# Lightning attention and mixture of depths on one core: who issues the second batch's stores, when the first fetch goes out, and in which order two score rows are compared

## The chip, the core and the metric

The kernel runs on one core of a Trainium2 chip. A core has five engines with instruction streams of their own: TensorE (PE in the profile; PEld is its loading of weights), VectorE (DVE), ScalarE (ACT), GpSimd (POOL) and SyncE (SP, which here only issues DMAs). They meet through semaphores. Each engine works through its own stream in order. The metric is the device time of one execution in microseconds, the median of the runs.

## The reference

The inputs are q, k and v of shape (4 batches, 8 heads, 768 positions, 64), a decay per head, a gate vector of 512, two weight matrices (512 x 1024 and 1024 x 512) and a capacity of 128.

```
for each block of 64 positions:
    out = ((q @ k.T) * Dmask) @ v  +  (q * lam_pow) @ kv_state
    kv_state = lam_block * kv_state + (k * rev_pow).T @ v
x = out with the heads side by side           # (4, 768, 512)
scores = x @ w_gate
for each batch: the 128 positions of highest score
    x[those] += sigmoid(scores) * (relu(x[those] @ w1) @ w2)
```

## The kernel before

**Tiling.** The 768 positions of a batch are six tiles of 128, so there are 24 tiles, numbered g = 0 to 23; batch 0 has tiles 0 to 5, batch 1 tiles 6 to 11, and so on. The main loop (L686) has one step for each tile, after a step -1. A step works on several tiles at once: it transposes q and k of tile g + 1 (`transposes`, L204, copied from PSUM by ScalarE at L208), multiplies the queries by the decay on GpSimd (`queries_decayed`, tile qs, L215 or L217), forms the scores of tile g + 1 (`scores`), the products of keys and values for the state (`state_products`, L279 or L288), the part of the output that comes from the state (`from_states`, L330 or L341) and the part that comes from the scores of tile g (`from_scores`, L357 or L364). ScalarE copies the outputs into the tile x_b (L386, or L392 and L394), which holds a whole batch. Steps up to 10 are "wide" (blocks of 128 positions at a time); from 11 on they are narrow (two blocks of 64), and they have time on TensorE for the experts' matrices (`expert`: L536, L572, L584), in pieces.

**Choosing the tokens.** `gate_scores` makes the score of each position on VectorE (xg, sc). `row` (L434 to L439) turns a tile's scores into a row: TensorE transposes them into a PSUM bank, ScalarE copies the row into sc_row in SBUF. `compare` (L441) counts on VectorE which scores beat which: a first comparison, `beat` (L447), reads `fresh[g]`; a second, `table` (L456), reads the rows of the earlier tiles from sc_row; L461 adds the two up. `column_sums` adds up the tables on TensorE (L473) and takes the result off the ranks (L477). Two steps after the end of a batch, `find` makes `hit` (L489), in which each position's rank is compared with the 128 places. `tokens` turns this into row numbers: six small matmuls on TensorE (L499) and two VectorE instructions (L504, L506). `fetch` (L523) is an indirect DMA, issued by GpSimd, that reads those 128 rows back from the output in HBM. `take` does both. The results of the experts are written over those rows by another indirect DMA (L602, L607).

**What sets the order.** The order in which instructions are given to each engine is written out by hand: it is the order of the calls. A row, a transposed tile and the products of L279 each take the next of four PSUM banks (`bank`), in turn, so a bank is written again only when the last reader of what it held is done. In steps 3 to 7 the dictionary `ROWS` says which rows are handled; step 7 takes two, those of tiles 5 and 6. Tile 6 is the first of its batch, so its comparison has no `table`. The row of a tile is therefore read twice by others than TensorE: by ScalarE's copy and by `beat`.

**DMAs.** SyncE issues all loads of k, q and v (L76, three for a tile, four to eight tiles ahead) and, in steps 8 to 13, the weights (L94 and L99). ScalarE issues the stores of finished tiles (L399), at the end of the steps that the dictionary `STORES` gives: tiles 6 and 7 in step 11, 8 and 9 in step 12, 10 and 11 in step 13. The framework gives DMAs of these two engines eight completion semaphores in turn, in an order over both engines. A DMA is issued only when the DMA that last used its semaphore has landed; that can be one of the other engine.

Of the kernel before, what the change touches and what calls it, by code (L numbers as in the profile page):

```python
# [17 lines left out]
def kernel(  # L18
# [12 lines left out]
    nc = tc.nc  # L31
# [5 lines left out]
    L = 128  # L37
    C = 64
    NT = S // L
# [103 lines left out]
    o_ = psum.tile([128, 2, 512], FP32, name="o")  # L143
    free = [psum.tile([128, 512], FP32, name=f"m{i}") for i in range(4)]
    held = []
    ROWS = {1: (), 2: (), 3: (0,), 4: (1, 2), 5: (3,), 6: (4,), 7: (5, 6)}
    KEPT = range(NG)
    STORES = {
        3: [0], 4: [1, 2], 5: [3, 4], 6: [5], 11: [6, 7], 12: [8, 9], 13: [10, 11], 18: [12, 13], 19: [14, 15], 20: [16, 17],
# [28 lines left out]
    def wide(g):  # L178
        return g < WIDE
# [44 lines left out]
    def scores(g, part=None):  # L224
        if g >= NG:
            return
        hps = range(NHP) if part is None else range(part * NHP // 2, (part + 1) * NHP // 2)
        qT, kT = qTs[g], kTs[g]
        if part != 0:
            qTs.pop(g), kTs.pop(g)  # L230
        if wide(g):
            to = o_ if part == 1 else su
            for hp in hps:
                for hh in range(2):
                    nc.tensor.matmul(  # L235
                        to[:, hh, hp * L : (hp + 1) * L], lhsT=kT[half[hh], hp, :],
                        rhs=qT[half[hh], hp, :], start=True, stop=True, skip_group_check=True,
                    )
            return
        for hp, hh, c in quarters():  # L240
            nc.tensor.matmul(  # L241
                su[half[c], hh, hp * C : (hp + 1) * C], lhsT=kT[half[hh], hp, half[c]],
                rhs=qT[half[hh], hp, half[c]], start=True, stop=True, skip_group_check=True,
            )
# [49 lines left out]
    def decay_state(n):  # L294
        g = n // 2
        if g >= NG or n % (2 * NT) == 0 or n % (2 * NT) == 2 * NT - 1:
            return
        if wide(g) and g % NT == NT - 1:
            return
        t = att.tile([128, NHP, D], FP32, name="decayed", bufs=2)  # L300
        nc.gpsimd.tensor_tensor(  # L301
            out=t[:], in0=states[n][:], in1=(decay_w if wide(g) else decay)[:], op=ALU.mult
        )
        decayed[n] = t
# [91 lines left out]
    def store(g):  # L396
        for n in STORES.get(g, [] if g in KEPT else [g]):
            b, t = divmod(n, NT)
            nc.scalar.dma_start(  # L399
                out=out[b, t * L : (t + 1) * L, :],  # L400
                in_=x_bs[b][:, t].rearrange("p a b e -> p (a b e)"),
            )
# [22 lines left out]
    def row(g):  # L425
        if not 0 <= g < NG:
            return
        b, t = divmod(g, NT)
        if t == 0:
            rows_[b] = mod.tile([128, S], FP32, name="sc_row")  # L430
            same_[b] = mod.tile([128, NT], FP32, name="same")
            prev_[b] = mod.tile([128, NT], FP32, name="prev")
            ranks[b] = mod.tile([128, NT], FP32, name="ranks")
        pb = bank()[:, :L]  # L434
        nc.tensor.transpose(  # L435
            pb, in_=scs[b][:, t : t + 1].broadcast_to([128, 128]), identity=ident[:]
        )
        nc.scalar.copy(out=rows_[b][:, t * L : (t + 1) * L], in_=pb)  # L438
        fresh[g] = pb  # L439

    def compare(g):  # L441
        if not 0 <= g < NG:
# [52 lines left out]
    def tokens(b, i):  # L495
        e = hits_.pop((b, i))
        pk = bank()[:, :2]
        for t in range(NT):
            nc.tensor.matmul(  # L499
                pk, lhsT=e[:, t, :], rhs=place[:, b * NT + t, :],  # L500
                start=(t == 0), stop=(t == NT - 1),
            )
        two = mod.tile([128, 2], FP32, name="two")
        nc.vector.tensor_copy(two[:], pk)  # L504
        tok = const.tile([128, 1], I32, name=f"tok{b}_{i}")
        nc.vector.scalar_tensor_tensor(  # L506
            out=tok[:], in0=two[:, 0:1], scalar=128.0, in1=two[:, 1:2],
            op0=ALU.mult, op1=ALU.add,
        )
        toks[b, i] = tok  # L510
# [10 lines left out]
    def fetch(b, i):  # L521
        xs = mod.tile([128, HD], FP32, name="xs")
        nc.gpsimd.indirect_dma_start(  # L523
            out=xs[:], out_offset=None, in_=rows_upto(b), in_offset=rows_at(b, i),
        )
        xss[b, i] = xs
# [142 lines left out]
    def ends(g):  # L669
        return g >= 0 and g % NT == NT - 1  # L670
# [5 lines left out]
    def take(b):  # L676
        for i in range(NGR):
            tokens(b, i)
            fetch(b, i)
# [6 lines left out]
    for g in range(-1, NG):  # L686
        loads_to(g + ahead(g), g)
        if g < 0:
            keys_decayed(0)
        if wide(g):  # L690
            if NGR:
                pending = list(tables)
                for n in ROWS.get(g, (g - 1,)):
                    row(n)
                    compare(n)
                for n in pending:
                    column_sums(n)
                if ends(g - 4):
                    take((g - 4) // NT)
            if g < 0:  # L700
                for part in range(2):
                    transposes(0, "kT", part)
                    transposes(0, "qT", part)
                for part in range(2):
                    scores(0, part)
                    masked(0, part)
                query_powers()
            elif g == 0:
                transposes(1, "kT")
                from_scores(0, 0)  # L710
                transposes(1, "qT")
                from_scores(0, 1)
                outputs(0)
                store(0)
                queries_decayed(1)
                nc.scalar.copy(
                    out=decay_w[:], in_=qpow[:, :, L - 1 : L].broadcast_to([128, NHP, D])
                )
                decay_state(2)
            else:  # L720
                for name in ("kT", "qT") if g == 1 else ("qT", "kT"):
                    transposes(g + 1, name)
                queries_decayed(g + 1)
                from_scores(g)
                outputs(g)
                store(g)
                if g > 1:
                    gate_scores(g)
            if g == 0:
                scores(1)  # L730
            if g != 1:
                state_products(g + 1)
            if g > 0:
                scores(g + 1)
            if wide(g + 1):
                from_states(g + 1)
            if g == 1:
                masked(g + 1)
                state_products(g + 1)
            if g < 0:  # L740
                keys_decayed(1)
                constants()
            else:
                keys_decayed(g + 2)
            if g == 0:
                masked(1)
            next_state(2 * g + 2)
            if g >= 0:
                decay_state(2 * g + (3 if not wide(g + 1) else 4))
            if g > 1:  # L750
                masked(g + 1)
            if g == 1:
                nc.scalar.copy(
                    out=wg_o[:].rearrange("p (a b e) -> p a b e", a=2, e=D),
                    in_=wg_b[:].rearrange("p (b a e) -> p a b e", a=2, e=D),
                )
            if g in (1, 2):
                gate_scores(g - 1)
            second(g + 1)
            if g == 3:  # L760
                casts()
                narrow_constants()
            if NGR and ends(g - 2):
                column_sums(g - 2)
                find((g - 2) // NT)
        else:
            transposes(g + 1, "qT")
            transposes(g + 1, "kT")
            if ends(g - 6):
                for i in range(NGR):  # L770
                    pieces.extend(expert((g - 6) // NT, i))
            products(1)
            from_states(g)
            settle(g)
            queries_decayed(g + 1)
            state_products(g + 1)
            next_state(2 * g + 2)
            decay_state(2 * g + 3)
            keys_decayed(g + 2)
            if NGR:  # L780
                column_sums(g - 2)
                if ends(g - 4):
                    take((g - 4) // NT)
                row(g - 1)
            products(1)
            second(g + 1)
            if NGR:
                compare(g - 1)
                if ends(g - 2):
                    find((g - 2) // NT)  # L790
            products(1)
            flush()
            from_scores(g)
            scores(g + 1)
            outputs(g)
            store(g)
            masked(g + 1)
            gate_scores(g)
# [55 lines left out]
```

## Time and profile before

| | |
|---|---|
| Median of 3 runs | 179.09 us (177.38 to 180.19) |
| The profiled execution, its own time | 178.91 us |
| Its span | 177.1 us |
| TensorE busy | 162.2 us (92%) |
| VectorE busy | 98.2 us (55%) |
| GpSimd busy | 85.6 us (48%) |
| ScalarE busy | 69.0 us (39%) |
| Moved by DMA | 32.20 MB in 82608 packets, mean 182 GB/s |
| Of these on SyncE's queue | 23.34 MB, 61.3% of 16 engines' span |
| On ScalarE's queue | 6.30 MB, 10.6% |
| On GpSimd's queue | 2.10 MB, 3.7% |

The profile is of one execution. A group of instructions is named by engine, line, the tile written and the tiles read. In the chain of waits each piece of time is put on what the last instruction of all was waiting for, step by step backwards; "issue" there is time in which the engine waited for nothing that the profile shows. In the timeline a line has the start, the duration, the engine, the line of the kernel, the operation with its tiles and sizes and, in brackets, how long the engine was idle before it and what ended that. ACTq, SPq and POOLq are instructions that the sequencer of the engine handles itself, such as issuing a DMA. A line of 40 digits shows how busy something was in 40 equal slices of the span, in tenths.

The narrow step 11 begins at about 60 us, step 12 at 67, step 13 at 74, step 14 at 81, step 15 at 89 and step 16 at 97 us, if a step's first transposes are taken as its beginning.

### The profile page before, as it was taken

Reading aid. Unit: us, or ns where it says so; the run is one execution under the profiler, and the core shown is the slowest. Engines: PE = TensorE matmul, PEld = TensorE weight load, DVE = VectorE, ACT = ScalarE, POOL = GpSimd, SP = SyncE. Lnnn points to the kernel's source line nnn. Section 1 sums busy time; section 2 is a strip of 40 time slices with the busy share of each in tenths; the row PEclk is TensorE's granted clock in tenths of the full one; section 3 lists DMA queues with packets and bytes.
Section 4 is the critical chain, followed back from the end, with each engine's and each line's share of the span. In section 5 each row is a group of like instructions: output and inputs, shape, how many; then the busy total and the mean of one; then the engine's idle time right before and its main releaser. Section 6 shows DMA issues by size and latency. Waiting matters only on the chain.

```text
span 177.1 us, 7473 instructions
## 1 busy us (share of the span) xinstructions
PE 162.2 (92%) x3228; PEld 133.9 (76%) x3228; DVE 98.2 (55%) x304; ACT 69.0 (39%) x173; POOL 85.6 (48%) x96
## 2 busy tenths in 40 slices
PE   7999899998998988999688999899998999999990
PEld 7788798886987877896365699787655699559970
DVE  2873479699885547545255668547565767030011
ACT  3345366444332623543521465545334353013100
POOL 1386965265459660863567564836856300202022
PEclk9999999999999999999999999999999999999998
DMA  4999999999999999899998999972134242201000
GB/s 106 224 225 215 198 235 241 251 277 240 220 222 269 299 254 246 275 311 254 276 258 188 249 233 210 199 186 82 44 122 130 103 155 95 63 0 59 0 30 30
DMA packets 82608, 32.20 MB, mean 182 GB/s; under 512 B 75792, under 2 KB 77840, under 8 KB 82576
## 3 DMA queue, kind: packets, MB, share of 16 engines
q1 hardware_dynamic: 78320, 23.34, 61.3%
q10 hardware_dynamic: 3600, 6.30, 10.6%
q0 software_dynamic: 656, 2.10, 3.7%
q8 instruction: 25, 0.41, 1.0%
q14 instruction: 7, 0.06, 0.1%
HBM read 24.38 MB, written 7.34 MB: 179 GB/s over the span
## 4 chain that ended last, share of the span: by engine, by line
PE 63%; issue 9%; DMA 8%; SPq 7%; POOL 6%; DVE 3%; ACT 2%; POOLq 1%; ACTq 1%; DVEq 0%
PE m L572 14%; PE m L584 12%; PE m L204 9%; SPq L76 5%; PE o L341 4%; PE o L357 4%; PE su L241 4%; DMA qn<-in_q_dram 4%; PE o L364 4%; DMA kn<-in_k_dram 4%; PE su L288 3%; PE su L235 2%; PE o L330 2%; PE m L435 2%; POOL kd L186 2%
## 5 line engine op out<-in xcount | busy, mean ns | idle before, releaser
L572 PE MATMUL m<-xsT,w_sb 128*128 128x128 f32 x256 | 31.4, 276 | 0.2 <-ACT kT L208 0.2
L572 PEld LDWEIGHTS m<-xsT,w_sb 128*128 128x128 f32 x256 | 29.9, 192 | 1.0 <-ACT xsT L541 0.6
L584 PE MATMUL m<-w_sb,hs 128*128 128x512 f32 (+1 forms) x80 | 30.1, 508 | 0.0
L217 POOL TENSOR_TENSOR qs<-qT,qpow 128x512 f32<-128x512 f32 x13 | 16.6, 1280 | 24.5 <-ACT qT L208 24.5
L301 POOL TENSOR_TENSOR decayed<-state,decay 128x256 f32<-128x256 f32 x21 | 16.7, 794 | 6.8 <-DVE ranks L477 6.4
L208 ACT COPY qT<-m 128x512 f32<-128x512 f32 (+1 forms) x25 | 14.2, 569 | 14.4 <-PE m L204 8.9
L584 PEld LDWEIGHTS m<-w_sb,hs 128*128 128x128 f32 x80 | 14.2, 193 | 5.6 <-issue 4.8
L320 DVE TENSOR_TENSOR state<-su,decayed 128x256 f32<-128x256 f32 x21 | 8.9, 424 | 14.4 <-POOL decayed L301 10.3
L438 ACT COPY sc_row<-m 128x128 f32<-128x128 f32 x24 | 6.2, 268 | 27.3 <-PE m L435 20.1
L208 ACT COPY kT<-m 128x512 f32<-128x512 f32 (+1 forms) x25 | 14.3, 573 | 6.4 <-PE m L204 6.1
L204 PE MATMUL m<-ident,qn 128*128 128x128 f32 x96 | 15.8, 285 | 0.7 <-DMA qn<-in_q_dram 0.7
L255 DVE TENSOR_TENSOR p<-su,mask_w 128x1024 f32<-128x1024 f32 (+1 forms) x11 | 12.9, 1171 | 5.4 <-PE su L235 5.4
L576 ACT ACTIVATE hs<-m 128x128 f32<-128x128 f32 x32 | 8.9, 279 | 17.8 <-PE m L572 17.3
L186 POOL TENSOR_TENSOR kd<-kn,kpow_w 128x512 f32<-128x512 f32 x11 | 11.4, 1041 | 8.7 <-DVE kpow_w L117 5.2
L204 PE MATMUL m<-ident,kn 128*128 128x128 f32 x96 | 15.2, 279 | 0.5 <-DVE beat L447 0.2
L215 POOL TENSOR_TENSOR qs<-qT,qpow 128x512 f32<-128x512 f32 x9 | 11.5, 1277 | 8.5 <-ACT qT L208 8.4
L186 POOL TENSOR_TENSOR kd<-kn,kpow 128x512 f32<-128x512 f32 x13 | 13.5, 1039 | 0.0
L241 PE MATMUL su<-qT,kT 64*64 64x64 f32 x416 | 10.1, 221 | 3.4 <-issue 1.7
L357 PE MATMUL o<-vn,p 128*64 128x64 f32 x352 | 12.9, 225 | 0.2 <-DVE p L255 0.2
L357 PEld LDWEIGHTS o<-vn,p 128*64 128x64 f32 x352 | 11.3, 138 | 2.2 <-issue 1.9
L204 PEld LDWEIGHTS m<-ident,kn 128*128 128x128 f32 x96 | 11.2, 143 | 1.6 <-DVE beat L447 1.1
L235 PE MATMUL su<-qT,kT 64*128 64x128 f32 x168 | 12.3, 285 | 0.1
(86 smaller groups left out, 271.6 us busy)
## 6 DMA issues: line engine op xcount, KB each, us to landing
vn<-in_v_dram SPq DMA_DIRECT2D x24, 256.0 KB, 5.4
out_dram<-x_b ACTq DMA_DIRECT2D x24, 256.0 KB, 4.1
kn<-in_k_dram SPq DMA_DIRECT2D x23, 256.0 KB, 5.7
qn<-in_q_dram SPq DMA_DIRECT2D x23, 256.0 KB, 6.4
w_sb<-in_moe_w_dram SPq DMA_DIRECT2D x4, 512.0 KB, 6.5
w_sb<-in_moe_w_dram SPq DMA_DIRECT2D x8, 256.0 KB, 5.8
kn<-in_k_dram SPq DMA_DIRECT2D x2, 128.0 KB
qn<-in_q_dram SPq DMA_DIRECT2D x2, 128.0 KB
```

Source lines behind the costliest of these rows:

```text
L186: nc.gpsimd.tensor_tensor(out=kd[:], in0=loaded[g][0][:], in1=pw[:].rearrange("p a b -> p (a b)").unsqueeze(2).broadcast_to([128, H, D]), ...
L204: nc.tensor.transpose(tp[:, hp * L : (hp + 1) * L], in_=t[:, 2 * hp : 2 * hp + 2, :], identity=ident[:])
L208: nc.scalar.copy(out=dsts[g][:].rearrange("p a i -> p (a i)")[:, at], in_=tp[:, at])
L215: nc.gpsimd.tensor_tensor(out=qs[:], in0=qTs[g][:], in1=qpow[:], op=ALU.mult)
L217: nc.gpsimd.tensor_tensor(out=qs[:].rearrange("p a (c i) -> p a c i", c=2), in0=qTs[g][:].rearrange("p a (c i) -> p a c i", c=2), in1=qpow ...
L235: nc.tensor.matmul(to[:, hh, hp * L : (hp + 1) * L], lhsT=kT[half[hh], hp, :], rhs=qT[half[hh], hp, :], start=True, stop=True, skip_group_ ...
L241: nc.tensor.matmul(su[half[c], hh, hp * C : (hp + 1) * C], lhsT=kT[half[hh], hp, half[c]], rhs=qT[half[hh], hp, half[c]], start=True, stop ...
L255: nc.vector.tensor_tensor(out=ps_[g][:, :, at], in0=(o_ if part == 1 else su)[:, :, at], in1=mask_w[:].rearrange("p a b i -> p a (b i)")[: ...
L301: nc.gpsimd.tensor_tensor(out=t[:], in0=states[n][:], in1=(decay_w if wide(g) else decay)[:], op=ALU.mult)
L357: nc.tensor.matmul(o_[half[c], hh, hp * D : (hp + 1) * D], lhsT=p[:, hh, i0 : i0 + C], rhs=vn[:, 2 * hp + hh, :], start=(hp == 0 and g % N ...
L572: nc.tensor.matmul(ph, lhsT=w1_sb[:, dc, f * 128 : (f + 1) * 128], rhs=keep["xsT"][:, dc, :], start=(dc == 0), stop=(dc == NDC - 1),)
L584: nc.tensor.matmul(py[:, e0:e1], lhsT=keep["hs"][:, f, :], rhs=w2_sb[:, f, e0:e1], start=(f == 0), stop=(f == NFC - 1),)
```

## The change

Three things are changed.

- The stores of batch 1 (tiles 6 to 11, in steps 11, 12 and 13) are issued by SyncE, in the same places of the written order. In SyncE's stream each pair stands after the weights of its step and before the loads of the next.
- `tokens` of batch 0 moves from the beginning of step 9 to step 8, behind the step's outputs and gate scores and ahead of its state products; `fetch` of batch 0 moves from the beginning of step 9 to step 8, after `decay_state`, which makes it the last thing that GpSimd does in that step. For the later batches `take` stays where it was.
- In step 7 row 6 is handled before row 5, and for these two rows `beat` reads ScalarE's copy in SBUF and no longer the PSUM bank.

```diff
-    ROWS = {1: (), 2: (), 3: (0,), 4: (1, 2), 5: (3,), 6: (4,), 7: (5, 6)}
+    ROWS = {1: (), 2: (), 3: (0,), 4: (1, 2), 5: (3,), 6: (4,), 7: (6, 5)}
@@ def store(g):
-            nc.scalar.dma_start(
+            (nc.sync if b == 1 else nc.scalar).dma_start(
                 out=out[b, t * L : (t + 1) * L, :],
@@ def row(g):
-        fresh[g] = pb
+        fresh[g] = rows_[b][:, t * L : (t + 1) * L] if g in ROWS[7] else pb
@@ the loop, wide steps
                 for n in pending:
                     column_sums(n)
-                if ends(g - 4):
-                    take((g - 4) // NT)
@@
             if g == 0:
                 scores(1)
+            if NGR and ends(g - 3):
+                for i in range(NGR):
+                    tokens((g - 3) // NT, i)
             if g != 1:
                 state_products(g + 1)
@@
             if g >= 0:
                 decay_state(2 * g + (3 if not wide(g + 1) else 4))
+            if NGR and ends(g - 3):
+                for i in range(NGR):
+                    fetch((g - 3) // NT, i)
             if g > 1:
                 masked(g + 1)
```

## The prediction, made before the changed kernel was run

> **What bounds the kernel now.** I read the page first: busy shares, the slices of the span, the chain that ended last. Then I read the timeline of each engine around the three places that the diff touches, and the waits of the built instruction lists.
>
> ```profile
> PE 162.2 (92%) x3228; PEld 133.9 (76%) x3228; DVE 98.2 (55%) x304; ACT 69.0 (39%) x173; POOL 85.6 (48%) x96
> PE   7999899998998988999688999899998999999990
> DMA  4999999999999999899998999972134242201000
> ```
>
> TensorE is busy for 92% of the span, so only its gaps can be won: 177.1 - 162.2 = 14.9 us in all. The DMA engines are full for the first 26 slices, that is to about 115 us. Up to there a second question is open: whether the loads would let TensorE go any faster. The weakest slice of TensorE before the tail is the twentieth (a 6, 84.1 to 88.6 us).
>
> ```profile
> 62.37 1.15 SPq L94
> 63.62 6.22 DMA kn<-in_k_dram
> 69.86 0.34 ACTq L399
> 70.34 0.44 issue
> 70.78 0.60 ACT kT L208
> 71.42 2.05 PE m L572 x16
> ...
> 79.94 1.41 POOL decayed L301
> 81.35 4.81 issue
> 86.20 1.26 POOL qs L217
> 87.46 0.69 POOL decayed L301
> 88.18 0.43 DVE state L320
> 88.75 0.69 PE su L241 x32
> ```
>
> This is the chain of waits. At 63.62 it goes through a load of keys, and then through a *store* on ScalarE, two things that share no data. The built lists say why: DMAs of SyncE and ScalarE take eight completion semaphores in turn, and each waits until the one eight before it has landed. The second store of step 11 comes eight after that load, and is issued 20 ns after the load lands. At 81.35 the chain has 4.81 us of "issue"; the timeline of ScalarE shows the same thing again:
>
> ```profile
> 81.54 0.74 ACT L394 COPY x_b<-o 64x256 f32<-64x256 f32 x2
> 84.59 0.83 ACTq L399 DMA_DIRECT2D out_dram<-x_b  x2
> 85.54 0.59 ACT L208 COPY qT<-m 128x512 f32<-128x512 f32 x1 [3.25 <-DVE state L320]
> ```
>
> ScalarE ends its copies at 82.28 and does nothing until the stores of step 13 go out. The keys load issued at 77.98 takes at most 6.5 us (the longest of that tile), 77.98 + 6.5 = 84.5: the store waits for it. The name after the arrow, DVE, had long been done. Behind the store are the copy of qT, GpSimd's qs and decayed, VectorE's state, and TensorE's scores at 88.75. Steps 7 and 9 have smaller holes:
>
> ```profile
> 43.67 0.34 DVE L447 SCALAR_TENSOR_TENSOR beat<-m,sc,lead 128x128 bf16<-128x128 f32 x1
> 44.12 0.69 PE L279 MATMUL m<-vn,kd 128*64 128x64 f32 x16 [0.56 <-POOL qs L215]
> ...
> 53.21 1.15 POOL L523 DMA_INDIRECT xs<-out_dram,tok  x1 [1.86 <-DVE tok L506]
> 54.39 1.27 POOL L215 TENSOR_TENSOR qs<-qT,qpow 128x512 f32<-128x512 f32 x1
> 54.60 0.59 ACT L386 COPY x_b<-o 128x512 f32<-128x512 f32 x1 [1.21 <-PE m L279]
> 56.07 0.69 PE L330 MATMUL o<-state,qs 64*64 64x64 f32 x32 [0.71 <-DVE sc L408]
> ```
>
> The L279 of step 7 writes a PSUM bank that still holds a score row; it starts when the second beat (43.67 to 44.02) has read that row. L330 of step 9 needs qs, which stands behind the fetch on GpSimd, and xg, which follows a late x_b.
>
> **What the Trainium skill says.** "DMA: Bandwidth & Descriptors", section "Issuing engines are not separate DMA queues": whichever engine starts a DMA, the same 16 DMA engines run it, and another issuer saves sequencer time alone. The trace agrees that all are shared (the DMA row is at 9 with stores and loads mixed), but here the sequencer time is the matter: 3.25 us of it on ScalarE. The same page, "Queues, rings and completion order": SP and ACT each own one row of rings, and an engine takes turns between rows. So a store among the loads stands in line with them, where before it took turns; of the loads in line, the store's bytes went before them in either case (step 11's second store, issued at 69.86, lands about 75, ahead of the next keys at about 77). "SBUF — State Buffer", "Who interferes with whom": a VectorE instruction with two SBUF inputs and a GpSimd one that reads SBUF shut each other out. The trace agrees: L461, two SBUF inputs, takes 0.16 us alone and 1.15 us at 42.60, until qs on GpSimd ends at 43.73.
>
> **Part 1, six stores to SyncE.** ScalarE loses six issues (0.34 us each, beside its copies) and, above all, their waits. Step 11: qT could be copied at 68.65 instead of 70.30. TensorE's idle 0.84 us before L435 (at 70.94) and 0.16 us before L572 (at 71.42) go: 1.00. Step 12: its stores held nothing (qT at 75.39 follows the copies): 0. Step 13: qT at 82.3, qs 83.0 to 84.3, decayed after the first state (85.1) to 85.9, the second state to 86.3; TensorE ends L364 at 87.15, so the 1.60 us before L241 go: 1.60. Sum 2.60. What is late next there is TensorE itself.
> On SyncE each pair is queued behind that step's w2 parts and ahead of the next kn, qn and vn. The stores' data was copied two to five steps earlier, so the wait on ScalarE is met. Their semaphores' previous users: for step 11 a vn and the last w1 part, landed by 66.1 and 68.9 in the landing records, and SyncE comes there at 70.6; for steps 12 and 13 earlier stores and a w2 part, also landed. Cost on SyncE: 0.34 to 0.63 us an issue (a store on ScalarE; a w2 part, 1.89 / 3, where the ring is full), 0.7 to 1.3 a pair. Cover: the loads behind have slack. Queries for step 14 land at 77.9 and are used at 81.51; for step 15, 85.7 and 89.37; for step 16, 92.6 and 97.33. That is 3.6 to 4.7 us. After all gains TensorE comes to the one of step 15 some 4 us sooner, 0.3 before they land. I charge 0.3; the bounds are 0 and 2.0 (a pair's issue not hidden at all, and a little more).
> The fetch of batch 1 (95.58, so about 91.6 after) needs these stores landed; before they landed at 88.7 and 90.4. About the same: 0.
>
> **Part 2, the two rows.** The same two transposes, two copies and all compares, in the order 6, 5. The first beats now wait for ScalarE's copies (41.38 and 41.55) and free both banks there. TensorE's 0.56 before L279 and about 0.06 before the kn transposes (41.76 to 41.82) go: 0.6. The price is that both beats have two SBUF inputs. GpSimd is idle from 41.05 to 42.46; beats from 41.41 end by about 42.3, just in time. If one misses, it waits 1.27 (a qs) on VectorE, which then delays xg and the next p: 0 to 1.3 on the path. I take 0.
>
> **Part 3, tokens and first fetch.** Six matmuls (0.16 us together) move from the start of step 9 into step 8: no net change on TensorE. Two VectorE instructions (0.15 + 0.16, the second perhaps waiting for a kd to end, up to 1.04) come ahead of step 8's state and p: p is about 0.4 us later, and in step 9 its user L357 comes 0.4 us after it, so nothing. That cover is thin. The order of banks turns with it: the kn transposes of step 9 no longer stand on a beat (0.1 us). The fetch goes out after decayed, about 51.1 to 52.3 on a clock moved by the step-7 gain, where GpSimd is idle; qs of step 10 then starts with its qT. L330's 0.71 goes if x_b comes in time. It was 0.81 later than the end of L357 (53.79 to 54.60), while the indirect DMA was on GpSimd. I cannot see why; if issuing it delays signals, that delay now falls on the row-8 transposes, whose copies have some slack. Bounds: -0.4 and +0.8 gained; I take 0.8.
>
> **Sum.** 2.60 + 0.6 + 0.8 - 0.3 = 3.7. The profiled execution took 178.91 us, with a span of 177.1 and so 1.8 around it; 178.91 - 3.7 = 175.2. Its time is 0.18 under the median of the runs shown, which is inside their spread. After 115 us nothing gives the gain back: DMA falls to 1 to 4 tenths, and TensorE is at 19.51 of 20.0 us between 121 and 141.
>
> **Rivals.** *The fetch brings nothing*: the late signal moves with it. Only part 3 is lost: about 176.1. For it: x_b at 54.60. Against it: copies there have slack.
> *Loads take the place of the stores' waits*: SyncE's pairs add up (2 us) and TensorE meets the loads of steps 14 to 16. Then 3.7 - 2.0: about 177.2. For it: DMA at 9 tenths and slack no greater than the gain. Against it: the same bytes went first before.
> *Slower: SyncE's line is held.* If a store on SyncE waits for a landing as the ones on ScalarE did, every load behind it waits too. Three pairs, each held for a store's landing (4.1 us), make 12.3 on the loads; less the slack of 3.7 at step 15, 8.6 on TensorE; less gains of 3.7, 4.9: about 183.8. It decides once holds add up to over 7.4. For it: vn at 81.50 already waited 1.2 for a landing. Against it: the semaphores named above are free by then.
>
> **Numbers.** Forecast 0.62 (its own range 174.0 to 176.0), fetch rival 0.12, loads 0.14, slower 0.12. Two per cent is about what a measurement of this kernel can tell from no change: faster means under 175.5. Of the forecast 0.54 lies below that, 0.08 above. So faster 0.54, same 0.08 + 0.12 + 0.14 = 0.34, slower 0.12. The range runs from 173.8 (no charge for loads, and 1 us of run spread) to 178.2 (the loads rival and the same spread).
>
> **What the profile after would show.** Part 1: ScalarE's qT of step 14 about 0.1 us after the copies, no wait over 1 us before qs there, no 6 in slice 20; the L399 of batch 1 on SyncE without idle before. Part 2: L279 of step 7 without a gap. Part 3: qs of step 10 straight after its qT, L330 without a gap. Wrong if: TensorE waits for qn or vn in steps 13 to 16, a beat of step 7 takes over 1 us, or x_b is late again.

## The result, and the profile after

| | before | after |
|---|---|---|
| Median of 20 runs each, on one chip | 179.27 us (177.38 to 180.95) | 177.81 us (175.32 to 182.07) |
| Ratio | | 0.989, 95% interval 0.986 to 0.992 |
| Profiled execution, its own time | 178.91 us | 180.74 us |
| Its span | 177.1 us | 179.0 us |

Medians are over all runs; a ratio compares only runs within 1.5% of the fastest of their kernel, so it is not the quotient of two medians. The changed kernel is about 1.1% faster, some 2 us, which is no difference at the 2% that was set. The forecast was 175.2 us, a gain of 3.7; the range, 173.8 to 178.2, holds the time. On two other chips the same change gave 0.999 (0.995 to 1.003) and 0.996 (0.992 to 1.001), so the gain lies between nothing and about 1%. The profiled execution of after is 2.9 us over the median of its kernel; it shows what holds the kernel, and a little more of it than most executions have.

The page of after, busy times and slices:

```profile
PE 163.3 (91%) x3228; PEld 134.8 (75%) x3228; DVE 97.8 (55%) x304; ACT 68.7 (38%) x173; POOL 85.6 (48%) x96
...
PE   7999899999999879998498999989998999999990
...
PEclk9999999999999999999969999999999999999999
DMA  4999899999999898999999998995133243201000
```

The 6 of before in the twentieth slice of TensorE is now a 4. It is not the same hole: the chain of waits of after, from 55 to 92 us, names another cause.

```profile
60.77 6.08 DMA qn<-in_q_dram
66.85 0.04 issue
66.89 0.67 PE m L204 x4
...
83.80 0.02 SPq L76
83.82 0.05 issue
83.87 6.00 DMA qn<-in_q_dram
89.87 0.04 issue
89.92 1.58 PE m L204 x8
```

No store is in it any more. Twice it runs from a load of queries straight into the transposes (L204) that use it. The timeline of TensorE, at the two holes that parts 2 and 3 were to close and at the new one:

```profile
44.06 0.64 PE L279 MATMUL m<-vn,kd 128*64 128x64 f32 x16
...
55.22 0.69 PE L330 MATMUL o<-state,qs 64*64 64x64 f32 x32
...
66.89 0.66 PE L204 MATMUL m<-ident,qn 128*128 128x128 f32 x4 [1.29 <-DMA qn<-in_q_dram]
...
89.92 0.72 PE L204 MATMUL m<-ident,qn 128*128 128x128 f32 x4 [2.68 <-DMA qn<-in_q_dram]
```

L279 of step 7 and L330 of step 9 start with no idle time (0.56 and 0.71 before). From 42 to 57 us TensorE is busy for 15.00 of 15.00 us, against 13.63 before. What follows is waiting for queries. The wait before 66.89 (for tile 13) comes before the first store on SyncE (73.34 below), so it is not the stores' doing: TensorE is sooner, and these queries were asked for at 60.77, before at 58.40. In the table of who waited for whom, in after:

```profile
POOL kd L186 <- DMA kn<-in_k_dram: 9.8, 6, 3.4
...
PE m L204 <- DMA qn<-in_q_dram: 6.4, 7, 2.7
```

Each line gives the us in total, the times and the longest. In the profile of before these totals are 1.8 and 0.7 us. SyncE's own timeline shows where the loads were meanwhile. After:

```profile
73.34 0.85 SPq L399 DMA_DIRECT2D out_dram<-x_b  x2
...
80.74 2.60 SPq L399 DMA_DIRECT2D out_dram<-x_b  x2
83.43 0.39 SPq L76 DMA_DIRECT2D kn<-in_k_dram  x1
83.87 0.78 SPq L76 DMA_DIRECT2D qn<-in_q_dram  x1
...
89.10 0.85 SPq L399 DMA_DIRECT2D out_dram<-x_b  x2
```

Before, the loads of the same tile (16):

```profile
77.98 0.38 SPq L76 DMA_DIRECT2D kn<-in_k_dram  x1
78.42 1.84 SPq L76 DMA_DIRECT2D qn<-in_q_dram  x1
```

The queries of tile 16 are asked for at 83.87 and not at 78.42, and land when TensorE has been idle for 2.68 us. Some 1.7 us of this delay are older than the stores (the queries of tile 14 were asked for at 66.03, before at 64.33), and in two later profiles of the same kernel tile 16 is asked for at 80.22 and 80.14: of the three this execution shows the largest delay. From 57 to 95 us SyncE's instructions follow each other in after with no hole over 0.42 us, so the profile shows no wait for a free buffer or a semaphore that holds the loads there, only the line. The last load of the kernel is issued at 118.2 us (112.2 before).

### The profile page after: what moved, and what is told of

It is laid out like the page before. It is cut to its first block, busy times and chain, and to the rows that moved or that the text cites. A ratio compares the mean times of both kernels' runs of the same rounds, so it can differ in the third digit from the quotient of the medians.

```text
span 179.0 us, 7476 instructions
## 1 busy us (share of the span) xinstructions
PE 163.3 (91%) x3228; PEld 134.8 (75%) x3228; DVE 97.8 (55%) x304; ACT 68.7 (38%) x173; POOL 85.6 (48%) x96
## 4 chain that ended last, share of the span: by engine, by line
PE 58%; SPq 19%; DMA 11%; issue 4%; POOL 2%; DVE 2%; ACT 1%; POOLq 1%; ACTq 1%
SPq L76 17%; PE m L572 15%; PE m L584 13%; PE m L204 7%; DMA qn<-in_q_dram 7%; PE o L364 4%; PE o L341 4%; PE su L241 3%; DMA vn<-in_v_dram 3%; PE su L288 3%; PE su L235 2%; PE o L357 2%; PE m L435 2%; SPq L94 2%; PE o L330 2%
## 5 line engine op out<-in xcount | busy, mean ns | idle before, releaser
L572 PE MATMUL m<-xsT,w_sb 128*128 128x128 f32 x256 | 31.3, 276 | 0.0
L584 PE MATMUL m<-w_sb,hs 128*128 128x512 f32 (+1 forms) x80 | 31.0, 520 | 0.0
L572 PEld LDWEIGHTS m<-xsT,w_sb 128*128 128x128 f32 x256 | 30.0, 193 | 0.6 <-ACT xsT L541 0.6
L204 PE MATMUL m<-ident,qn 128*128 128x128 f32 x96 | 15.6, 284 | 6.4 <-DMA qn<-in_q_dram 6.4
L584 PEld LDWEIGHTS m<-w_sb,hs 128*128 128x128 f32 x80 | 14.5, 197 | 5.6 <-issue 4.5
L204 PEld LDWEIGHTS m<-ident,qn 128*128 128x128 f32 x96 | 10.4, 142 | 8.0 <-DMA qn<-in_q_dram 6.6
L576 ACT ACTIVATE hs<-m 128x128 f32<-128x128 f32 x32 | 8.9, 278 | 18.0 <-PE m L572 17.5
L204 PE MATMUL m<-ident,kn 128*128 128x128 f32 x96 | 15.5, 284 | 0.3 <-ACT kT L208 0.2
L341 PEld LDWEIGHTS o<-state,qs 64*64 64x64 f32 x384 | 7.6, 139 | 6.6 <-issue 3.9
```

The lines of the kernel that those rows point to most:

```text
L204: nc.tensor.transpose(tp[:, hp * L : (hp + 1) * L], in_=t[:, 2 * hp : 2 * hp + 2, :], identity=ident[:])
L341: nc.tensor.matmul(o_[half[hh ^ c], hh, hp * D : (hp + 1) * D], lhsT=qs[half[hh], hp, half[c]], rhs=states[n][half[hh], hp, :], start=(hp ...
L572: nc.tensor.matmul(ph, lhsT=w1_sb[:, dc, f * 128 : (f + 1) * 128], rhs=keep["xsT"][:, dc, :], start=(dc == 0), stop=(dc == NDC - 1),)
L584: nc.tensor.matmul(py[:, e0:e1], lhsT=keep["hs"][:, f, :], rhs=w2_sb[:, f, e0:e1], start=(f == 0), stop=(f == NFC - 1),)
```

## The experiments

Ratios are to the kernel before on the same chip, with the 95% interval. The kernel before against itself gave 0.996 (0.992 to 1.000), so less than about 0.4% is not told apart.

**The parts taken alone.** Part 1 is the line of `store` alone; parts 2 and 3 are the rest of the diff. The expectations weigh three theories, called L, F and N in the first of them. Beside the parts on the chip, the changed kernel again, and a version with weights asked for later, to clear the way for the loads of tiles 13 to 16:

```diff
-    WEIGHTS = {8: 1, 9: 2, 10: 1, 11: 3, 12: 3, 13: 2}
+    WEIGHTS = {8: 1, 9: 1, 10: 1, 11: 1, 12: 3, 13: 3, 14: 2}
```

> Part 1 alone: the six stores on SyncE, the rest as before. Theory L (the three gains are real, but together they bring TensorE up to the loads, which then set the pace): alone this part stays inside the loads' slack, so nearly its whole 2.6 us, about 176.7 and a ratio of 0.985. Theory F (the stores in SyncE's line delay the loads behind them): the delay eats it, about 178.5, ratio 0.995 or nearer to 1, with waits of the query transposes on their loads in this profile. Theory N (the gaps that I counted were not all lost time): in between, without waits on loads.

> Parts 2 and 3 alone: rows in the order 6, 5 from the copy, tokens and fetch a step sooner; stores as before on ScalarE. L: 1.4 us, about 177.9, ratio 0.992, and with part 1 alone more than the whole change gives. F: 1.4 us too, but the sum with part 1 alone is then what the whole change gives. N: under 0.7 us.

> The changed kernel once more, beside the others on one chip: about 177.3, ratio 0.989, under every theory. L and F: waits of the transposes on loads of q in steps 12 to 16, several us in all.

> The changed kernel with the weights asked for later: in steps 8 to 14 one, one, one, one, three, three and two parts (before one in 8, two in 9, one in 10, three, three and two in 11 to 13). The loads of tiles 13 to 16 then have one w1 part or three w2 parts fewer ahead of them, about 2.3 to 2.7 us. L: most of the lost gain comes back, about 175.5, ratio 0.979, and the transposes' waits on loads are gone or under 1 us. N: no change from the changed kernel, 177.3. F: some of it comes back, since the stores still stand ahead of the loads: about 176.5.

Measured: part 1 alone 0.999 (0.995 to 1.003), parts 2 and 3 alone 0.997 (0.993 to 1.001), all three 0.999 (0.995 to 1.003), weights later 1.030 (1.023 to 1.038). No part shows its own gain, and the changed kernel none here. L's ratios are all missed. Part 1 came out as F had it: no gain, and waits for queries (the table further below). The last run doesn't decide anything on the loads: its waits for queries fell, but now a piece of weights came 5.57 us late for L584. It was a badly chosen experiment.

**Weights put off evenly, and half of v.** The milder edit of the weights, in both kernels; the unchanged kernel once more; and the load itself made smaller: from tile 8 on only heads 0 to 3 of v are loaded, and used for all heads, so these two kernels leave out half of v (the last diff has only the loading; the matmuls that read v are changed to match).

```diff
-    WEIGHTS = {8: 1, 9: 2, 10: 1, 11: 3, 12: 3, 13: 2}
+    WEIGHTS = {8: 1, 9: 1, 10: 1, 11: 1, 12: 4, 13: 4}
```

```diff
             order = [(0, front), (1, front), (0, back), (1, back), (2, whole)]
+        if g >= 8:
+            order[2] = (2, front)
```

> The kernel before, once more, as a measure of what no change gives: ratio 1.000, and its profile shows how late loads come on this chip. Theory L (the loads of tiles 13 to 16 set the pace; the store on ScalarE waited for a load that TensorE needs a few us later in any case): TensorE takes some 87 us from the first transposes of tile 16 to the end, whatever the kernel, and here these transposes start within 2 us of the landing of their q. Theory N (the counted gaps were not lost time): they start over 3 us after it, as in the first profile, where 3.7 us lay between.

> The changed kernel with weights in steps 8 to 13 as one, one, one, one, four and four parts, so that none is asked for behind the loads of tiles 17 and 18. The loads of tiles 14 and 15 have one w1 part, and two or more w2 parts, fewer ahead of them, some 2 us. L: the transposes of tile 16 about 2 us sooner than in the changed kernel, no wait of L584 on w2 over 1 us: ratio to before about 0.985. N or F (the stores in SyncE's line are what delays): the same time as the changed kernel.

> The same weights in the kernel before. L: it gains too, about 1 us (0.994), since the store on ScalarE waits for a keys load that now lands sooner; less than the changed kernel gains. N: nothing, 1.000.

> The changed kernel with only the first four heads of v loaded for tiles 8 to 23, and used again for the other four (so the second four heads' outputs from tile 8 on are other numbers); every instruction of the engines stays, the loads carry a sixth less there. L: waits of TensorE on loads under 1 us, and a time about 4 us under before: 0.977. N: no more than the changed kernel's gain, 0.99 or nearer to 1, since loads don't matter.

> The kernel before with only the first four heads of v loaded for tiles 8 to 23, used for all eight (the second four heads' outputs from tile 8 on are other numbers). The changed kernel with these lighter loads was at 0.974. L and F: the change is worth more where loads don't bind, about 2 us, so this one is at 0.985. N (the counted gaps were not lost time): 0.975, as fast as the changed one.

| | ratio | 95% interval |
|---|---|---|
| changed, weights even | 0.997 | 0.993 to 1.002 |
| before, weights even | 1.009 | 1.005 to 1.014 |
| changed, half of v | 0.974 | 0.968 to 0.979 |
| before, half of v (on another chip) | 1.000 | 0.996 to 1.003 |

The weights again settle nothing: in before they made it slower, which no theory had. The other pair does. With lighter loads the kernel before gains nothing, against both expectations: its limit lies elsewhere, and its profile still has TensorE waiting 1.06 and 1.01 us behind ScalarE's stores. The changed one goes to 0.974 (six runs), and after 20 us no wait of TensorE for queries reaches 0.3 us. So the holes that the change closes were lost time, worth about what was forecast or more (2.6% is 4.6 us, by the interval 3.7 to 5.6) once loads are out of the way. That excludes the rival reading that the holes cost nothing.

**Which step puts the loads off?** Two ways of keeping the stores out of SyncE's line. In one they stay on ScalarE but are issued a step later, behind the copies of qT and kT; in the other GpSimd issues them.

```diff
+    LATER = (11, 12, 13)
...
             transposes(g + 1, "kT")
+            if g - 1 in LATER:
+                store(g - 1)
...
-            store(g)
+            if g not in LATER:
+                store(g)
```

```diff
-            (nc.sync if b == 1 else nc.scalar).dma_start(
+            (nc.gpsimd if b == 1 else nc.scalar).dma_start(
```

> Parts 2 and 3 of the change; the stores of batch 1 stay on ScalarE's queue, but are issued one step later, behind the copies of qT and kT of the next tile, so that what waits for them is no longer qT. Theory F (a store in SyncE's line delays every load behind it by about its own transfer, 0.9 us, while on a queue of its own it runs beside the loads): loads land as in the kernel before (q of tile 16 near 85 us, last load issued near 113), and the gain of the stores' part comes without its price: ratio to before about 0.985. Theory L alone (loads set the pace, whoever issues the stores): as the whole change, 0.995, with waits of the transposes on q of several us.

> The kernel before with the stores of batch 1 deferred in the same way, nothing else. F: better than the stores on SyncE alone gave, ratio 0.99, loads as in the kernel before. L alone: 0.997.

> The changed kernel with the stores of batch 1 issued by GpSimd in place of SyncE. F: loads land as in the kernel before (q of tile 16 near 85 us), since the stores have a queue of their own again; the time depends on what six issues cost on GpSimd, where qs stands behind each pair: about 0.99 if a pair costs under 1 us there, 1.00 if 2 us. L alone: loads as late as in the changed kernel.

Measured: parts 2 and 3 with deferred stores 0.990 (0.987 to 0.994); the kernel before with deferred stores 1.006 (1.002 to 1.010); the changed kernel with its stores on GpSimd 0.984 (0.977 to 0.992). Deferring moves the wait: TensorE's L572 then waits up to 2.46 us for hs (ScalarE's L576), which stands behind the stores. Parts 2 and 3 with it lie between F's 0.985 and L's 0.995; for the kernel before both theories are missed. With GpSimd's stores there is no such wait, and the loads stay as early as in before (the last is issued at 112.4 us).

**Side by side on one chip.**

> The changed kernel as it is, for the same chip as the next three. F (six stores in SyncE's line put off the loads behind them): slower than the version with GpSimd's stores by 0.7 to 1.5 per cent, that is 0.988 to 0.999 of the kernel before. If SyncE's line costs nothing: the same as that version within 0.4 per cent.

> The changed kernel with batch 1's stores issued by GpSimd. F: 0.98 to 0.988 of the kernel before; the last load is issued at about 112 us and not at 116 to 118, and TensorE waits for queries under 1 us at tiles 16 and 17. If SyncE's line costs nothing: as the changed kernel.

> The kernel before with batch 1's stores issued by GpSimd: part 1 without SyncE's line. F with all else as predicted: the gaps of 1.0 and 1.6 us go and no load is put off, so 2.6 us or 0.985. If the loads stop it anyhow, because TensorE is then that much nearer to them: 0.990 to 0.997. If the waits on ScalarE weren't what held the path: 1.00.

> Parts 2 and 3 alone, batch 1's stores on ScalarE as before. By the prediction's terms 0.6 and 0.8: 0.992. If the store's wait on ScalarE, which is a wait for a load, takes back what TensorE has won by then: 0.996 to 1.00. The changed kernel should be no faster than this by more than 0.3 per cent if part 1 brings nothing in SyncE's line.

| batch 1's stores | kernel | median (before: 176.87) | ratio | last load issued | q of tile 17 issued |
|---|---|---|---|---|---|
| SyncE | changed | 175.93 us | 0.996 (0.992 to 1.001) | 118.3 us | 88.58 us |
| GpSimd | changed | 173.49 us | 0.990 (0.983 to 0.997) | 112.6 us | 84.78 us |
| GpSimd | before | 175.23 us | 0.990 (0.985 to 0.995) | 114.8 us | 87.36 us |
| ScalarE | parts 2 and 3 | 176.14 us | 0.998 (0.993 to 1.003) | 113.5 us | 85.91 us |

The intervals of the first two rows overlap. Set against each other directly, the runs behind these ratios have a mean of 174.9 us with SyncE's stores (14 runs, 173.47 to 176.04) and 173.2 with GpSimd's (6 runs, 171.88 to 174.12), some 1% apart. Few runs; where the loads stand says more. Busy times by stretch, 57 to 90 us, the columns after PE, PEld, DVE, ACT and POOL being the granted clock, the share of the DMA engines and GB/s. Stores on SyncE, the changed kernel of this chip:

```profile
57.00:90.00 33.00, 29.47 (x756) 24.66 (x754) 17.82 (x59) 14.77 (x39) 19.92 (x19) 1.00 1.02 263
```

Stores on GpSimd:

```profile
57.00:90.00 33.00, 30.70 (x753) 25.26 (x752) 18.65 (x61) 14.52 (x38) 22.82 (x26) 1.00 1.07 280
```

In the same stretch before has 276 GB/s and after 244. Over all profiles (those with half of v left out) it is 244 to 263 in the six kernels whose stores SyncE issues and 260 to 286 in the twelve others. So with the stores in a queue of their own, ScalarE's or GpSimd's, more bytes move in the same time. The share of 1.07 against 1.02 says that packets overlap more on the engines. The order of landing shows it too. On SyncE the two stores of step 12 land at 84.50 and 85.22, and only then the keys (86.24) and queries (87.35) of tile 16. With GpSimd's stores the keys land at 83.61, a store at 84.32, the queries at 85.22, the other store at 85.89: the stores run between the loads. The timelines of the two kernels at tile 16 and 17, first the changed one:

```profile
78.71 0.85 SPq L399 DMA_DIRECT2D out_dram<-x_b  x2
...
80.14 1.62 SPq L76 DMA_DIRECT2D qn<-in_q_dram  x1
...
87.14 0.85 SPq L399 DMA_DIRECT2D out_dram<-x_b  x2
...
88.58 1.23 SPq L76 DMA_DIRECT2D qn<-in_q_dram  x1
...
87.39 0.66 PE L204 MATMUL m<-ident,qn 128*128 128x128 f32 x4 [2.04 <-DMA qn<-in_q_dram]
95.58 0.66 PE L204 MATMUL m<-ident,qn 128*128 128x128 f32 x4 [1.90 <-DMA qn<-in_q_dram]
```

and with GpSimd's stores:

```profile
79.20 1.12 POOL L399 DMA_DIRECT2D out_dram<-x_b  x2
...
78.92 0.87 SPq L76 DMA_DIRECT2D qn<-in_q_dram  x1
...
84.78 1.08 SPq L76 DMA_DIRECT2D qn<-in_q_dram  x1
...
85.26 0.66 PE L204 MATMUL m<-ident,qn 128*128 128x128 f32 x4 [0.36 <-DMA qn<-in_q_dram]
```

A pair takes GpSimd 1.1 to 1.2 us, and TensorE has no idle time behind it. Of the two waits of about 2 us one is gone and one at 0.36. This version is the fastest here that loads all of v: 0.984 and 0.990, with a profiled span of 170.1 us. In time that is 2.8 and 1.8 us, still short of the 3.7 that were forecast.

**Parts 2 and 3 one by one** (each is its lines of the diff).

> Part 2 alone (rows 6 and 5 in turn, first beats from the copy). By the term: 0.6 us, 0.9965; TensorE's gap of 0.56 before L279 of step 7 gone. If tile 13's queries take it back: 1.00, with a wait for them at L204.

> Part 3 alone (tokens and first fetch a step sooner). By the term: 0.8 us, 0.9955; TensorE's gap of 0.71 before L330 of step 9 gone. If the signal from TensorE to ScalarE is late wherever the indirect DMA is issued: the gap is at another place and the ratio is 1.00.

Measured: part 2 alone 0.999 (0.995 to 1.003), part 3 alone 1.015 (1.005 to 1.024). Each closes its own hole and leaves the other: in the run of part 2, 0.62 us before L330 remain and none before L279; in that of part 3, 0.55 before L279 and none before L330. In both a new hole opens in step 12. Timelines of ScalarE and TensorE in the run of part 2:

```profile
76.36 1.40 ACTq L399 DMA_DIRECT2D out_dram<-x_b  x2
77.87 0.58 ACT L208 COPY qT<-m 128x512 f32<-128x512 f32 x1 [4.11 <-DMA kn<-in_k_dram]
...
78.51 0.32 PE L435 MATMUL m<-ident,sc 128*128 128x128 f32 x1 [2.25 <-ACT qT L208]
```

and in that of part 3:

```profile
77.19 1.52 ACTq L399 DMA_DIRECT2D out_dram<-x_b  x2
78.83 0.59 ACT L208 COPY qT<-m 128x512 f32<-128x512 f32 x1 [3.75 <-DMA kn<-in_k_dram]
...
79.47 0.48 PE L435 MATMUL m<-ident,sc 128*128 128x128 f32 x1 [1.90 <-ACT qT L208]
```

TensorE comes to step 12 sooner, and the stores of that step, which before were issued without a wait, now stand on ScalarE for a load of keys. Why part 3 alone is slower and not merely no faster stays open: the two profiles are alike, and it has six runs.

All of this in one table: TensorE's idle times of 0.5 us and more at these three places, by profile, in us. The first 40 us, where most kernels wait up to 0.7 us for queries at about 18 us, are left out.

| kernel | steps 7 and 9 | for queries, L204 | behind ScalarE's stores (L435, L241) |
|---|---|---|---|
| before | 0.56, 0.71 | none | 0.84, 1.60 |
| before, again | 0.56 | 0.72 | 1.73, 2.14 |
| part 2 | 0.62 | 0.86 | 0.66, 2.25, 1.03 |
| part 3 | 0.55 | none | 0.75, 1.90, 0.56 |
| parts 2 and 3 | none | 1.26 | 0.84, 1.43 |
| parts 2 and 3, side by side | none | 0.96 | 1.07, 2.36 |
| part 1 | 0.56 | 1.08, 0.86, 1.35, 1.28 | none |
| changed | none | 0.52, 1.29, 1.03, 2.68 | none |
| changed, again | none | 1.22, 0.85, 1.73 | none |
| changed, side by side | none | 1.02, 2.04, 1.90 | none |
| before, GpSimd's stores | 0.56 | none | none |
| changed, GpSimd's stores | none | 0.74 | none |
| the same, its first run | none | none | none |

The last two columns add up to 2.4 to 5.5 us in every kernel of the table whose stores are issued by ScalarE or by SyncE, and to 0.7 or nothing with GpSimd. The first wait for queries of a row (0.72 to 1.29, between 64 and 67 us, and in one row 0.52 at 59.8) is there with any of the three engines as the issuer, and on SyncE before its first store. What comes after the first store on SyncE is 2.6 to 3.9 us.

## Why the prediction was wrong in size

The direction was right; of the 3.7 us that were forecast 2.0 came on the first chip, 0.2 and 0.7 on two others. The steps, in the order of the prediction:

- **Stores off ScalarE, 2.60.** Right in mechanism. No wait behind stores is left in after, and the kernel before with GpSimd's stores alone gains 1.0%, about 1.8 us (0.9 to 2.6 by the interval). Whether the term was too large is not shown.
- **"The store's bytes went before them in either case", with "I charge 0.3; the bounds are 0 and 2.0".** This is the step that failed. It priced only the issuing of a pair, 0.7 to 1.3 us (0.85 in most, but 1.79 and 2.60 in two), against the slack of the loads, and gave the store's bytes no price at all. Here a store in a queue of its own did not go before the loads but beside them, at a higher rate in all (280 GB/s against 263 on one chip). The Trainium skill's "DMA: Bandwidth & Descriptors", section "Queues, rings and completion order", says that an engine takes turns between the rows that have work; the prediction cited it and drew the wrong conclusion. In SyncE's line six stores put the load stream off by 3.5 to 5.7 us at its end (118.3 against 114.8, 113.5 and 112.6 on one chip). At tiles 16 and 17 that is more than the slack that is left, and after the first of these stores TensorE waits 2.6 to 3.9 us for queries, not 0.3. In time the line costs some 1.1 to 1.7 us on that chip (0.996 against 0.990; 174.9 us against 173.2). So another issuer changed more than the sequencer's time, against what the prediction took. The rest of the shortfall stays open: with GpSimd's stores 0.9 to 1.9 us are still lacking.
- **"What is late next there is TensorE itself."** Wrong: the queries of tiles 16 and 17 are. They were among the loads whose slack the prediction had worked out as 3.6 to 4.7 us, "no greater than the gain". It carried the gain to step 15 (tile 16), but not the delay of the loads with it, and neither of them to step 16.
- **"Step 12: its stores held nothing: 0."** True of the execution of before. But the wait is there as soon as TensorE is sooner: 2.25 and 1.90 us. So parts 2 and 3 without part 1 gave no gain clear of the spread (0.997 and 0.998), and the terms could not simply be added up.
- **Part 2, 0.6.** Mechanism right. The beats read the copy, take 0.35 us each, and L279 has no gap. The price feared, a beat shut out by GpSimd, did not come.
- **Part 3, 0.8.** Mechanism right, size too large. Of the eight profiles with the fetch in its old place four have a late x_b (ScalarE idle for 1.2 us before it) and 0.62 to 0.71 us before L330; in the other four ScalarE is idle for 0.45 and L330 waits 0.37 or 0.38, behind qs. That is 0.5 us on average, and the profile before was one of the bad half. In all twelve profiles with the fetch moved x_b comes 0.41 us after ScalarE came free (in after at 53.75), and L330 has no gap. So the rival that the late signal moves with the fetch falls. Why the signal is late in half of the executions stays open.
- **The rivals.** "Loads take the place of the stores' waits", 177.2 us, is nearest to what happened; it took a price of 2.0 us where the forecast took 0.3, and had a chance of 0.14. "SyncE's line is held" did not happen: the semaphore instruction ahead of a store on SyncE takes 17 ns, though one store's issue took 2.12 us. "After 115 us nothing gives the gain back" held: in after no wait of TensorE for a load reaches 0.3 us there.
- **Slips in the working.** The lower end of the range comes to 173.9 and not 173.8 (175.2 less 0.3 and 1). And the 3.25 us on ScalarE, called sequencer time, are a wait for a load to land; an issue took 0.34.

## What to carry to other kernels

Moving a DMA off a busy engine's queue has two prices: its issue, and its bytes in the line that it joins. Ask which transfers stand behind it there, and carry their delay and the time won together to the step that uses them. Where several holes lie one behind the other, closing one is worth only the distance to the next wait: test edits together as well as one by one, and try a queue on which nothing urgent stands behind the transfer.

## What the runs showed that was not expected

**A wait of 1.9 us can be followed by 1.7 us of missing clock.** Eight of the twenty profiles have, before the last 10 us, a stretch in which TensorE's granted clock is at half, always just after or during a long idle time. In after, by stretches of 2 us (the clock is the third column from the end):

```profile
88.00:90.00 2.00, 0.09 (x1) 0.09 (x2) 0.69 (x2) 0.00 (x0) 1.03 (x2) 1.00 0.85 183
90.00:92.00 2.00, 2.00 (x9) 1.62 (x10) 0.00 (x0) 1.00 (x2) 1.31 (x3) 0.59 1.00 344
92.00:94.00 2.00, 2.00 (x41) 0.87 (x42) 0.00 (x0) 0.17 (x1) 0.65 (x1) 0.55 1.07 249
94.00:96.00 2.00, 2.00 (x51) 1.34 (x44) 1.39 (x6) 0.27 (x1) 0.78 (x2) 1.00 1.17 221
```

Added up, the clock missing is 1.71 us in five of them and 3.42 in three, that is 3.42 us, or twice that, at half speed; the three are those with the longest idle times, 2.70, 3.56 and 5.57 us. The Trainium skill's "TensorE: Matmul & The Clock Gate", section "Part 1: The HAM clock gate", gives these two speeds and a free-running window of 3413 ns, and the trace agrees. It names an idle window of about 3.4 us as the condition, and there the trace differs: 1.90 us (part 3, and the changed kernel at 95.58) was followed by half speed, while 2.04, 2.14, 2.36 and 2.46 us in four other places were not. No step of the prediction had this price. It goes with a part of the spread between executions: of 21 executions of the changed kernel on the first chip, the nine with a mean clock of 0.990 or less have a median of 179.2 us, the other twelve 176.9.

**"Issue" inside a run of matmuls.** Some stalls of TensorE have no releaser: 2.70 us before 81.02 in the kernel before with GpSimd's stores, 0.78 to 1.33 at the same place in the stream in five others. In each the DMA packets show a block of instructions (queue 8, 16 KB) landing 1.5 to 1.7 us before TensorE goes on: 79.37 for 81.02, 77.15 for 78.78, 78.20 for 79.80. The same holds, with 1.2 to 1.7 us, for all 31 stalls of this kind over 0.5 us in the twenty profiles. So TensorE seems to wait there for its own instructions, while the DMA engines are full of loads. That was seen, not tested. This stall and the 3.42 us of clock missing around it are what is large in the profile of before with GpSimd's stores (span 175.7 us), in which no wait of 0.5 us for loads or stores is left.
